# Two score passes moved in front of w_in and quads prepared one further ahead: cosine attention with a GELU MLP

## The chip, the cores and the metric

The kernel runs on one core of a Trainium2 chip. The metric is the device time of one execution in microseconds (us); the medians come from several executions. The profile is of one more execution, recorded by the hardware profiler. The engines are called PE (TensorE), DVE (VectorE), ACT (ScalarE), POOL (GpSimd) and SP (SyncE, which here only issues DMAs).

## What is computed

```python
# q, k, v: (8 batches, 12 heads, 448 positions, 64), tau = 0.1
q_n = q / (norm(q, axis=-1) + 1e-6)
k_n = k / (norm(k, axis=-1) + 1e-6)
attn = softmax(q_n @ k_n^T / tau)
x = concat_heads(attn @ v)              # (8*448, 768)
h = x @ w_in                            # (3584, 2048)
out = (0.5 * h * (1 + erf(h / sqrt(2)))) @ w_out   # (3584, 768)
```

Inputs and output are float32. The kernel multiplies in bfloat16 and accumulates in float32. Since the normalised scores are bounded by 1 / tau = 10, it takes exponentials without subtracting the maximum.

## The kernel before, in words

**Units of work.** Four heads of a batch make a quad, so a batch has NQ = 3 quads and the kernel 24 (numbered 0 to 23; batch b has quads 3b, 3b+1, 3b+2). Quad 0 is split in two, so unit numbers (`units`, line 112) are quad numbers plus one from quad 1 on.

**Preparation of a quad**, in steps over several engines: `load_qk` (line 122, two DMAs issued on SP), `square` (147, on POOL), `reduce` (158, on DVE: sums of squares), `logs` and `roots` (169 and 174, on ACT: square root as exp(0.5 ln)), `inverses` (183: an addition on POOL, a reciprocal on DVE), `scale` (200, two multiplications on POOL giving bfloat16), and `transposes` (214, one DMA transpose issued on SP into `qkT`). `root` (195) is logs, roots and inverses in a row. The three steps of a root work on a *group* of one or two units (`groups`, 114), so that one logarithm serves both. Buffers limit how far ahead a quad can be: `qk` has four, `qkb` and `qkT` three each, `sq` two.

**Attention of a batch.** A *pass* is one quad's scores for one chunk c of 64 keys for both head pairs (`scores`, 236: four quarter-array matmuls into a pair of PSUM banks), and its exponential on ACT (`exps`, 250). A quad has seven passes, a batch 21. There are three pairs of banks, 0, 1 and 2. `both` (325) ends a quad: `sums` (259, row sums by matmuls with ones, into the next of the two remaining banks), their transposition, inversion and spreading on DVE, `values` (278, attention times v, into one of the pairs), and `normalise` (321, on DVE, writes x).

**MLP of a batch.** `first` (630) multiplies x with w_in: 16 blocks m of 128 features with six matmuls (kd) each, and a Gelu on ACT for each block. The first `ahead` blocks run their first four kd before the last two, which need the last quad of x. Blocks sit in pairs of banks as `pairs` says, else in the two single banks in turn. Exponential and Gelu need different tables on ACT, so `first` loads the Gelu table at its start and the other at its end.

The second product is cut into pieces of 16 matmuls (`second_pieces`, 346), with a copy on DVE (line 356) and two stores on SP at the end. Pieces take the two single banks in turn, so a piece waits for the copy of the piece before the last. These matmuls, one at a time, are the `fill` of the next batch's attention: 96 in odd batches, 128 in even ones.

**The order of the work** is written out by hand: the program has a manual schedule, and each engine executes its instructions in the order in which the Python code issues them. `attention_first` (405) is the first batch. `attention(b, fill)` (584) alternates `run()`, which issues the next so many w_out matmuls of `plan`, with groups of passes (`group`, 578, from the table `group_pairs`: passes 3, 3, 3, 2, 3, 3, 2, 2, each with the pairs that it uses). The first group of a batch is issued at the end of `first` of the batch before. `upto(f, n)` (394) issues step f for all units below n that have not had it; where it stands decides where the step lies in its engine's queue.

Of the kernel before, what the change touches and what calls it, by code (L numbers as in the profile page):

```python
# [16 lines left out]
def kernel(  # L17
# [20 lines left out]
    NQ = H // 4  # L38
# [66 lines left out]
    def pair(i, name):  # L105
        pool = third[0] if i == 2 else ps_st
        return pool.tile([128, 2, 512], F32, tag=f"st{i}", name=name)
# [3 lines left out]

    units = [(0, 0, 1), (0, 1, 2)] + [(g, 0, 2) for g in range(1, NG)]
    NU = len(units)
    groups = [[n] for n in range(NQ + 2)] + [[NQ + 2, NQ + 3]]
    for n in range(2 * NQ + 1, NU, NQ):
        groups += [[n, n + 1], [n + 2]]
    shapes = [[len(gr), 2, units[gr[0]][2] - units[gr[0]][1], C] for gr in groups]
    place = {u: (n, j) for n, gr in enumerate(groups) for j, u in enumerate(gr)}
    qk_t, v_t, sq_t, nq_t, rn_t, qkb_t, qkT_t, pt_t = {}, {}, {}, {}, {}, {}, {}, {}
# [139 lines left out]
    def sums(g, chunks=range(C)):  # L259
        for c in chunks:  # L260
            if c == 0:
                bank_t[g, "sm"] = ps_acc.tile([128, 512], F32, tag="sm", name=f"sm{g}") if g < NQ else \
                    mm_tile(f"sm{g}", aside=0)
            for s in range(2):
                if g < NQ:
                    nc.tensor.matmul(bank_t[g, "sm"][64 * s:64 * (s + 1), :S],  # L266
                                     lhsT=ones2.rearrange("p a h r -> p (a h r)"), rhs=pt_t[g, s, c],
                                     start=(c == 0), stop=(c == C - 1), tile_position=(0, 64 * s))
                    continue

                half = 2
                for i in range(2) if c == half else ((c - (c > half)) % 2,):
                    r = 32 * (2 * s + i)
                    cols = slice(i * S // 2, (i + 1) * S // 2) if c == half else slice(0, S)
                    nc.tensor.matmul(bank_t[g, "sm"][r:r + 32, cols], lhsT=ones, rhs=pt_t[g, s, c][:, cols],  # L275
                                     start=(c < 2), stop=(c >= C - 2), tile_position=(0, r))
# [18 lines left out]
    def turned(g):  # L295
        tr = rcp.tile([128, NB, 32], F32, tag="tr", name=f"tr{g}")
        nc.vector.transpose(tr.rearrange("p b r -> p (b r)"), bank_t.pop((g, "sm"))[:, :S])  # L297
        bank_t[g, "tr"] = tr.rearrange("p b (k r) -> p k b r", k=2)

    def inverted(g):  # L300
        tr = bank_t.pop((g, "tr"))
        if g < NQ:
            su = tr[:, :, :, 0]
        else:


            for j in range(4):
                o = j ^ 1
                nc.vector.tensor_reduce(tr[32 * j:32 * (j + 1), :, :, 1], tr[32 * o:32 * (o + 1), :, :, 0:1],  # L309
                                        mybir.AxisListType.X, ALU.add)  # L310
            su = rcp.tile([128, 2, NB], F32, tag="su", name=f"su{g}")
            nc.vector.tensor_reduce(su, tr[:, :, :, 0:2], mybir.AxisListType.X, ALU.add)
        rc = bank_t[g, "rc"] = rcp.tile([128, 2, NB], F32, tag="rc", name=f"rc{g}")
        nc.vector.reciprocal(rc, su)

    def spread(g, h):
        rs = rcp.tile([128, NB, 32], F32, tag=f"rs{h}", name=f"rs{g}_{h}")
        nc.vector.transpose(rs, bank_t[g, "rc"][:, h].to_broadcast([128, NB, 32]))  # L318
        rs_t[g, h] = rs.rearrange("p b r -> p (b r)")
# [5 lines left out]
    def both(g, p):  # L325
        sums(g)
        turned(g)
        inverted(g)
        spread(g, 0)
        spread(g, 1)  # L330
        values(g, p=p)
        normalise(g, 0)
        normalise(g, 1)
# [60 lines left out]
    def upto(f, n, last=None):  # L394
        last = {load_qk: NG, load_v: NV, root: len(groups), load_wi: 4, load_wo: 4}.get(f, NU)
        while done.get(f, 0) < min(n, last):
            done[f] = done.get(f, 0) + 1
            f(done[f] - 1)
# [173 lines left out]
        done.update({square: 6, reduce: 5, root: 5, scale: 5, transposes: 5})  # L572


    passes = [(n, c) for n in range(NQ) for c in range(C)]
    group_pairs = [(0, 1, 2), (0, 1, 2), (0, 1, 2), (1, 2), (1, 2, 0), (1, 2, 0), (2, 0), (2, 0)]

    def group(b, k):
        n0 = sum(len(p) for p in group_pairs[:k])
        for p, (n, c) in zip(group_pairs[k], passes[n0:]):  # L580
            scores(b * NQ + n, ((0, c), (1, c)), p)
            exps(b * NQ + n, ((0, c), (1, c)))

    def attention(b, fill):
        fill = list(fill)
        plan = {96: (20, 13, 13, 12, 16, 22), 128: (24, 18, 20, 18, 22, 26)}[len(fill)]
        parts = iter(plan)

        def run():
            for _ in range(next(parts)):  # L590
                fill.pop(0)()

        x_t[b] = xp.tile([128, KD, S], BF16, tag="x", name=f"x{b}")
        g0, nu = b * NQ, (b + 1) * NQ + 1
        run()
        for n in (nu - 1, nu):
            upto(scale, n)
            upto(transposes, n)
        group(b, 1)
        upto(square, nu + 1)  # L600
        run()
        group(b, 2)
        both(g0, 0)
        upto(load_v, b + 3)
        if b == 1:
            upto(load_qk, g0 + NQ + 2)
        group(b, 3)
        upto(square, nu + 2)
        run()
        group(b, 4)  # L610
        upto(reduce, nu + 1)
        upto(load_qk, g0 + NQ + 3)
        run()
        group(b, 5)
        both(g0 + 1, 1)
        group(b, 6)
        run()
        group(b, 7)
        upto(reduce, nu + 2)
        n = 2 * b + 4  # L620
        if n < len(groups):
            logs(n)
            roots(n)
        run()
        both(g0 + 2, 1)
        if n < len(groups):
            inverses(n)
            done[root] = n + 1

    def first(b):  # L630
        sb, hf = divmod(b, 2)
        if hf == 0:
            g_t[sb] = gp.tile([128, KF, 2 * S], BF16, tag="g", name=f"g{sb}")
        nc.scalar.preload_act_table_set(GELU_SET)
        nu = (b + 1) * NQ + 1
        hps = {}
        pairs = (0, 2) if b else (0, 2, 6, 8)
        ahead = 4 if b else 5

        def mm(m, kds):  # L640
            for kd in kds:
                nc.tensor.matmul(hps[m], lhsT=wi[:, kd, m * 128:(m + 1) * 128],  # L642
                                 rhs=x_t[b][:, kd, :], start=(kd == 0), stop=(kd == KD - 1))

        def bank(m):
            if m in pairs:
                p = (2, 0)[m // 2] if b else (1, 0, 1, 0)[pairs.index(m)]
                st = pair(p, f"hp{b}_{m}")
                hps[m], hps[m + 1] = st[:, 0, :S], st[:, 1, :S]
            elif m not in hps:  # L650
                hps[m] = mm_tile(f"hp{b}_{m}")[:, :S]

        for m in range(ahead):
            bank(m)
            mm(m, range(KD - 2))
        if b == 0:
            upto(square, nu + 3)
        for n in (nu + 1, nu + 2) if b else (nu + 1,):
            upto(scale, n)
            upto(transposes, n)  # L660
        if b:
            upto(load_qk, (b + 1) * NQ + 5)
        else:
            upto(load_wo, 4)
        upto(square, nu + 3)
        upto(reduce, nu + 3)
        for m in range(ahead):
            mm(m, range(KD - 2, KD))
        for m in range(KF):
            if b == 0 and m == 8:  # L670
                for i in range(2):
                    transposes(4, i)
                    copies(4, i)
            if m >= ahead and (m == 0 or m - 1 not in pairs):
                for k in range(m, m + 1 + (m in pairs)):
                    bank(k)
                    mm(k, range(KD))
            nc.scalar.activation(g_t[sb][:, m, hf * S:(hf + 1) * S], hps.pop(m), AF.Gelu)  # L678
            if b == 0 and m == 5:
                nc.scalar.preload_act_table_set(EXP_SET)  # L680
                upto(root, 6)
                nc.scalar.preload_act_table_set(GELU_SET)
                upto(scale, nu + 2)
                upto(transposes, nu + 2)
                upto(load_qk, 2 * NQ + 1)
        if b + 1 < B:
            nc.scalar.preload_act_table_set(EXP_SET)
            group(b + 1, 0)
            upto(root, 2 * b + 6)

    upto(load_qk, 1)
    nc.scalar.preload_act_table_set(EXP_SET)
# [7 lines left out]
    fill = []  # L700
    for b in range(B):
# [12 lines left out]
        fill = [f for t, ni in todo if t not in tail for f in second_pieces(sb, t, ni)]  # L714
# [38 lines left out]
```

## Time and profile before

| | |
|---|---|
| median of 3 runs | 417.64 us (417.42 to 418.03) |
| the profiled execution | 418.57 us, span from first to last instruction 416.8 us |
| first batch's attention | 0 to 33.4 us |
| w_in of batches 0 and 1 | 33.4 to 52.5 and 80.6 to 98.9 us |
| one exponential of a pass | 917 ns, 168 of them |
| one Gelu | 547 ns, 128 of them |
| one square of a quad on POOL | 3.17 us |
| one reduction of a quad on DVE | 2.0 us |

Part 1 of the page has the busy time of each engine; part 4 the chain of work that ended last, followed back from the last instruction. [...] In the lists in order of time the first column is the start and the second the length, in us. An idle time in brackets names what ended it.

### The profile page before, as it was taken

The numbers are of one execution on the slowest core, as the hardware profiler recorded it, in microseconds if no ns is written. First come the engines' busy times: TensorE is split into PE (matmuls) and PEld (weight loads), VectorE is DVE, ScalarE is ACT, GpSimd is POOL, SyncE is SP. The second block draws the span as 40 slices with busy tenths as digits, with TensorE's granted clock in tenths as the row PEclk, the third lists the DMA queues.
The fourth block names the chain that finished last, engine by engine and source line by source line (L and its number), as shares of the span: only waits on it lengthen the run. The fifth ranks groups of instructions, "written<-read, shape, count | busy, mean of one in ns | idle before, by whom it ended". The sixth has DMA issues, their size and how long they took to land.

```text
span 416.8 us, 8254 instructions
## 1 busy us (share of the span) xinstructions
PE 409.3 (98%) x3506; PEld 212.1 (51%) x3506; DVE 188.3 (45%) x379; ACT 246.6 (59%) x358; POOL 167.3 (40%) x113
## 2 busy tenths in 40 slices
PE   7899999999999999999999999999999999999996
PEld 3344545555555554554555555455555554555564
DVE  5777228801676016741276314861167511661021
ACT  5995698356663578735865359735866348844300
POOL 4999706090900909053640636317280272000000
PEclk9999999999999999999999999999999999999999
DMA  8999999445473546729192382936375160430033
GB/s 288 263 259 205 204 215 258 115 81 186 91 185 77 92 174 92 187 60 242 18 233 65 77 228 43 195 77 126 141 135 180 38 90 0 85 75 2 0 77 76
DMA packets 66516, 54.53 MB, mean 131 GB/s; under 512 B 38576, under 2 KB 61488, under 8 KB 66480
## 3 DMA queue, kind: packets, MB, share of 16 engines
q1 hardware_dynamic: 53984, 41.79, 39.3%
q0 software_dynamic: 12112, 11.80, 17.8%
q8 instruction: 27, 0.44, 0.4%
q10 hardware_dynamic: 384, 0.43, 0.3%
q14 instruction: 9, 0.07, 0.1%
HBM read 45.61 MB, written 11.01 MB: 136 GB/s over the span
## 4 chain that ended last, share of the span: by engine, by line
PE 95%; DMA 2%; ACT 1%; DVE 1%; SPq 1%; issue 0%; DVEq 0%
PE hp L642 35%; PE op L352 35%; PE st L246 9%; PE o L289 8%; PE sm L275 4%; DMA qk<-in_q_dram 2%; PE op L367 1%; PE sm L266 1%; ACT pt L253 1%; SPq L129 1%; PE tp L225 0%; DVE qkT L230 0%; ACT sq L154 0%; DVE rn L192 0%; ACT root L178 0%
## 5 line engine op out<-in xcount | busy, mean ns | idle before, releaser
L253 ACT ACTIVATE pt<-st 128x896 bf16<-128x896 f32 x168 | 143.0, 917 | 39.6 <-PE st L246 38.7
L352 PE MATMUL op<-wo,g 128*128 128x384 bf16 x864 | 147.9, 327 | 0.0
L642 PE MATMUL hp<-x,wi 128*128 128x448 bf16 x768 | 146.8, 353 | 0.0
L678 ACT ACTIVATE g<-hp 128x448 bf16<-128x448 f32 x128 | 66.8, 547 | 99.3 <-PE hp L642 99.0
L352 PEld LDWEIGHTS <-g 128*128 128x128 bf16 x864 | 81.1, 98 | 63.2 <-issue 12.7
L642 PEld LDWEIGHTS <-wi 128*128 128x128 bf16 x768 | 74.4, 98 | 71.4 <-issue 2.9
L208 POOL TENSOR_TENSOR qkb<-qk,rn 128x896 bf16<-128x896 f32 (+1 forms) x49 | 79.7, 1652 | 47.1 <-DVE rn L192 47.1
L165 DVE TENSOR_REDUCE nq<-sq 128x28 f32<-128x1792 f32 (+2 forms) x30 | 48.8, 1637 | 64.6 <-POOL sq L156 61.3
L156 POOL TENSOR_TENSOR sq<-qk 128x1792 f32<-128x1792 f32 (+1 forms) x22 | 66.8, 3042 | 12.9 <-DMA qk<-in_k_dram 12.7
L356 DVE COPY ot<-op 128x384 f32<-128x384 f32 x54 | 29.5, 547 | 69.6 <-PE op L352 69.6
L190 POOL TENSOR_SCALAR se<-sr 128x28 f32<-128x28 f32 (+1 forms) x14 | 4.4, 313 | 122.7 <-ACT sr L181 122.7
L246 PE MATMUL st<-qkT 64*64 64x448 bf16 x672 | 48.3, 359 | 1.2 <-DVE qkT L230 1.0
L289 PE MATMUL o<-pt,v 64*64 64x448 bf16 x672 | 36.9, 352 | 0.0
L246 PEld LDWEIGHTS <-qkT 64*64 64x64 bf16 x672 | 18.2, 105 | 26.6 <-issue 18.3
L192 DVE RECIPROCAL rn<-se 128x28 f32<-128x28 f32 (+2 forms) x18 | 6.8, 376 | 51.4 <-POOL se L190 51.1
L318 DVE STREAM_TRANSPOSE rs<-rc 128x448 f32<-128x448 f32 x48 | 28.1, 623 | 0.8
L297 DVE STREAM_TRANSPOSE tr<-sm 128x448 f32<-128x448 f32 x24 | 15.6, 649 | 28.5 <-PE sm L275 25.4
L323 DVE TENSOR_TENSOR x<-o,rs 128x448 bf16<-128x448 f32 x48 | 27.0, 600 | 1.0 <-DVE rs L318 0.5
L289 PEld LDWEIGHTS <-v 64*64 64x64 bf16 x672 | 17.7, 106 | 15.8 <-issue 7.2
L275 PE MATMUL sm<-pt,ones 128*32 128x448 bf16 (+1 forms) x336 | 19.3, 332 | 0.0
L309 DVE TENSOR_REDUCE tr<-tr 32x28 f32<-32x28 f32 x84 | 16.5, 196 | 1.6
L275 PEld LDWEIGHTS <-ones 128*32 128x32 bf16 x336 | 7.4, 95 | 10.6 <-issue 8.9
(43 smaller groups left out, 118.5 us busy)
## 6 DMA issues: line engine op xcount, KB each, us to landing
out_dram<-ot SPq DMA_DIRECT2D x54, 192.0 KB, 2.7
qk<-in_q_dram SPq DMA_DIRECT2D x23, 448.0 KB, 6.3
qk<-in_k_dram SPq DMA_DIRECT2D x23, 448.0 KB, 7.0
v<-in_v_dram POOLq DMA_DIRECT2D x7, 672.0 KB, 10.8
wi<-in_moe_w_in_dram POOLq DMA_DIRECT2D x8, 384.0 KB, 14.3
wo<-in_moe_w_out_dram POOLq DMA_DIRECT2D x4, 768.0 KB, 14.0
qk<-in_q_dram SPq DMA_DIRECT2D x2, 224.0 KB, 3.6
v<-in_v_dram POOLq DMA_DIRECT2D x1, 448.0 KB, 9.5
```

The costliest lines, as they stand in the source:

```text
L156: eng.tensor_tensor(sq[:, part], t[:, part], t[:, part], ALU.mult)
L165: nc.vector.tensor_reduce(nq[:, part], sq[:, part], mybir.AxisListType.X, ALU.add)
L208: eng.tensor_tensor(qkb[:, i, :, s0:s1].rearrange("p c s d -> p s c d"), t[:, i, s0:s1], rn[:, i].to_broadcast([128, s1 - s0, C, D]), ALU. ...
L246: nc.tensor.matmul(st[cols, n, :S], lhsT=qkT[rows, 1, c, cols], rhs=qkT[rows, 0, :, cols], start=True, stop=True, tile_position=(64 * s, 6 ...
L253: nc.scalar.activation(pt[:, :m], st[:, :m, :S], AF.Exp, scale=inv_tau)
L275: nc.tensor.matmul(bank_t[g, "sm"][r:r + 32, cols], lhsT=ones, rhs=pt_t[g, s, c][:, cols], start=(c < 2), stop=(c >= C - 2), tile_position ...
L289: nc.tensor.matmul(bank_t[g, h][cols, :S], lhsT=v_t[g][rows, s, c, :], rhs=pt_t[g, s, c][rows], start=(c == 0), stop=(c == C - 1), tile_po ...
L318: nc.vector.transpose(rs, bank_t[g, "rc"][:, h].to_broadcast([128, NB, 32]))
L352: nc.tensor.matmul(ps[:, :NH], lhsT=g_t[sb][:, kf, t * 128:(t + 1) * 128], rhs=wo[:, kf, ni * NH:(ni + 1) * NH], start=(kf == 0), stop=(kf ...
L356: nc.vector.tensor_copy(ot[:, ni * NH:(ni + 1) * NH], ps[:, :NH])
L642: nc.tensor.matmul(hps[m], lhsT=wi[:, kd, m * 128:(m + 1) * 128], rhs=x_t[b][:, kd, :], start=(kd == 0), stop=(kd == KD - 1))
L678: nc.scalar.activation(g_t[sb][:, m, hf * S:(hf + 1) * S], hps.pop(m), AF.Gelu)
```

## The change

The passes of a batch b of 2 or more come in another order: two passes stand behind the values at the end of the attention of batch b - 1, in front of `first(b - 1)`; then follow, with w_out matmuls in between, 3, 3, 3, 3 with `both` and 2 more, and 3 with `both` and 2 more. In the words of the change, 2, 3, 3, 3, 5, 5. Batch 1 still begins with three passes behind `first(0)`, then 3, 3, 2, 3 with both and 2, 3 with both and 2. `plan` has other numbers of matmuls, as many runs as before. Quads 0 and 1 of a batch used to share a root; now the third quad of a batch and the first of the next do, and the second stands alone. The first quad of the next batch is scaled and transposed during the attention before, where it was done in `first`. In batch 1 a block of its own issues reduce, root, scale and transposes of quad 6 behind its third group of three passes, the one at the end of `first(0)` counted. In `first`, for b of 1 or more, blocks 0 and 1 take the single banks, blocks 2 to 5 take pairs 0 and 1, and six blocks run ahead instead of four.

```diff
-    groups = [[n] for n in range(NQ + 2)] + [[NQ + 2, NQ + 3]]
-    for n in range(2 * NQ + 1, NU, NQ):
-        groups += [[n, n + 1], [n + 2]]
+    groups = [[n] for n in range(NQ + 2)] + [[NQ + 2, NQ + 3], [2 * NQ + 1]]
+    for n in range(2 * NQ + 2, NU, NQ):
+        groups += [[n], [n + 1, n + 2] if n + 2 < NU else [n + 1]]
...
-    group_pairs = [(0, 1, 2), (0, 1, 2), (0, 1, 2), (1, 2), (1, 2, 0), (1, 2, 0), (2, 0), (2, 0)]
-
-    def group(b, k):
-        n0 = sum(len(p) for p in group_pairs[:k])
-        for p, (n, c) in zip(group_pairs[k], passes[n0:]):
+    at = {}
+
+    def visit(b, pairs):
+        for p in pairs:
+            n, c = passes[at.get(b, 0)]
+            at[b] = at.get(b, 0) + 1
             scores(b * NQ + n, ((0, c), (1, c)), p)
             exps(b * NQ + n, ((0, c), (1, c)))
...
-        plan = {96: (20, 13, 13, 12, 16, 22), 128: (24, 18, 20, 18, 22, 26)}[len(fill)]
+        plan = {96: (16, 14, 16, 18, 16, 16), 128: (20, 18, 20, 22, 32, 16)}[len(fill)]
...
-        g0, nu = b * NQ, (b + 1) * NQ + 1
+        g0, u = b * NQ, b * NQ + 1
         run()
-        for n in (nu - 1, nu):
-            upto(scale, n)
-            upto(transposes, n)
-        group(b, 1)
-        upto(square, nu + 1)
+        upto(scale, u + 3)
+        upto(transposes, u + 3)
+        if b == 1:
+            upto(load_qk, g0 + NQ + 2)
+            upto(square, u + 4)
+        visit(b, (0, 1, 2))
+        if b > 1:
+            upto(scale, u + 4)
+            upto(transposes, u + 4)
         run()
-        group(b, 2)
+        visit(b, (0, 1, 2))
+        if b == 1:
+            upto(reduce, u + 4)
+            upto(root, 2 * b + 5)
+            upto(scale, u + 4)
+            upto(transposes, u + 4)
+        run()
+        upto(load_qk, g0 + NQ + 3)
+        visit(b, (0, 1) if b == 1 else (0, 1, 2))
+        upto(square, u + 5)
+        run()
+        visit(b, (0, 1, 2))
         both(g0, 0)
         upto(load_v, b + 3)
-        if b == 1:
-            upto(load_qk, g0 + NQ + 2)
-        group(b, 3)
-        upto(square, nu + 2)
+        upto(load_qk, g0 + NQ + 4)
+        visit(b, (1, 2))
+        upto(reduce, u + 5)
         run()
-        group(b, 4)
-        upto(reduce, nu + 1)
-        upto(load_qk, g0 + NQ + 3)
-        run()
-        group(b, 5)
+        visit(b, (1, 2, 0))
         both(g0 + 1, 1)
-        group(b, 6)
-        run()
-        group(b, 7)
-        upto(reduce, nu + 2)
-        n = 2 * b + 4
+        visit(b, (2, 0))
+        n = 2 * b + 5
         if n < len(groups):
             logs(n)
             roots(n)
         run()
-        both(g0 + 2, 1)
+        both(g0 + 2, 2)
         if n < len(groups):
             inverses(n)
             done[root] = n + 1
+            visit(b + 1, (0, 1))
...
-        pairs = (0, 2) if b else (0, 2, 6, 8)
-        ahead = 4 if b else 5
+        pairs = {2: 0, 4: 1} if b else {0: 1, 2: 0, 6: 1, 8: 0}
+        ahead = 6 if b else 5
...
-        for n in (nu + 1, nu + 2) if b else (nu + 1,):
-            upto(scale, n)
-            upto(transposes, n)
-        if b:
+            upto(square, u + 3)
+            upto(scale, u + 1)
+            upto(transposes, u + 1)
+            upto(load_wo, 4)
+            upto(reduce, u + 3)
+        else:
+            upto(scale, u + 2)
+            upto(transposes, u + 2)
             upto(load_qk, (b + 1) * NQ + 5)
-        else:
-            upto(load_wo, 4)
-        upto(square, nu + 3)
-        upto(reduce, nu + 3)
+            upto(square, u + 4)
+            upto(reduce, u + 4)
...
-            group(b + 1, 0)
-            upto(root, 2 * b + 6)
+            if b == 0:
+                visit(1, (0, 1, 2))
+            else:
+                upto(root, 2 * b + 7)
```

More of the change, by code (lines that the diff above doesn't have):

```diff
@@ L634, in first @@
         nc.scalar.preload_act_table_set(GELU_SET)
-        nu = (b + 1) * NQ + 1
+        u = (b + 1) * NQ + 1
         hps = {}
-        pairs = (0, 2) if b else (0, 2, 6, 8)
-        ahead = 4 if b else 5
+        pairs = {2: 0, 4: 1} if b else {0: 1, 2: 0, 6: 1, 8: 0}
+        ahead = 6 if b else 5
         def mm(m, kds):
@@ L646, in bank @@
             if m in pairs:
-                p = (2, 0)[m // 2] if b else (1, 0, 1, 0)[pairs.index(m)]
-                st = pair(p, f"hp{b}_{m}")
+                st = pair(pairs[m], f"hp{b}_{m}")
                 hps[m], hps[m + 1] = st[:, 0, :S], st[:, 1, :S]
@@ L656, in first @@
         if b == 0:
-            upto(square, nu + 3)
-        for n in (nu + 1, nu + 2) if b else (nu + 1,):
-            upto(scale, n)
-            upto(transposes, n)
-        if b:
+            upto(square, u + 3)
[6 more added lines that the diff above has]
+            upto(transposes, u + 2)
             upto(load_qk, (b + 1) * NQ + 5)
-        else:
-            upto(load_wo, 4)
-        upto(square, nu + 3)
-        upto(reduce, nu + 3)
+            upto(square, u + 4)
+            upto(reduce, u + 4)
         for m in range(ahead):
@@ L682, in first @@
                 nc.scalar.preload_act_table_set(GELU_SET)
-                upto(scale, nu + 2)
-                upto(transposes, nu + 2)
+                upto(scale, u + 2)
+                upto(transposes, u + 2)
                 upto(load_qk, 2 * NQ + 1)
```

## The prediction

> **What bounds the kernel now.** I read the busy times first, then the chain that ended last, then that chain in order of time.
>
> ```profile
> PE 409.3 (98%) x3506; PEld 212.1 (51%) x3506; DVE 188.3 (45%) x379; ACT 246.6 (59%) x358; POOL 167.3 (40%) x113
> PE 95%; DMA 2%; ACT 1%; DVE 1%; SPq 1%; issue 0%; DVEq 0%
> ```
>
> TensorE is busy 98% of the span and 95% of the chain is its own. The waits of TensorE show none after 53 us. So from the second batch on nothing is gained by shortening another engine's work: time comes only from TensorE's own pauses between kinds of matmul, or goes if the change lets TensorE wait. The chain in order of time (start, length, what) shows these pauses; first an odd batch (96 w_out matmuls), then the last w_out pieces, then the second batch (b = 1).
>
> ```profile
> 147.99 2.27 PE hp L642 x12
> 150.26 0.69 PE st L246 x12
> 150.95 3.36 PE op L352 x20
> 154.31 0.82 PE st L246 x12
> 155.12 2.22 PE op L352 x13
> 157.34 0.72 PE st L246 x12
> 158.06 0.98 PE sm L275 x16
> ...
> 392.19 15.60 PE op L352 x96
> ```
>
> ```profile
> 53.18 3.36 PE op L352 x20
> 56.53 0.82 PE st L246 x12
> ```
>
> 96 w_out matmuls straight behind w_in take 15.60 us, 0.1625 each. Behind a score group 20 take 3.36, so 0.11 us is the way from quarter tiles to full ones. Three passes take 0.69 between w_out runs, where each pass alone is 0.187 (two take 0.38 directly behind values, 0.50 behind w_out): 0.13 is the way back. The first sums of a batch take 0.98 (1.01 in even batches) where later ones take 0.78: their last chunk waits for an exponential. The 0.82 is a third pass waiting for its PSUM pair.
>
> Second, what the moved preparation hangs on in batch 1, from the timelines of GpSimd, ScalarE and VectorE (start, length):
>
> ```profile
> 62.00 3.17 POOL L156 TENSOR_TENSOR sq<-qk 128x1792 f32<-128x1792 f32 x1 [11.26 <-DMA qk<-in_k_dram]
> 65.12 0.90 POOL L141 DMA_DIRECT2D v<-in_v_dram  x1
> ```
>
> ```profile
> 65.60 2.00 DVE L165 TENSOR_REDUCE nq<-sq 128x28 f32<-128x1792 f32 x1
> ```
>
> ```profile
> 103.19 0.33 ACT L172 ACTIVATE lq<-nq,tiny 128x28 f32<-128x28 f32 x1
> 103.61 0.23 ACT L181 ACTIVATE sr<-lq 128x28 f32<-128x28 f32 x1
> ```
>
> ```profile
> 103.92 0.28 POOL L190 TENSOR_SCALAR se<-sr 128x28 f32<-128x28 f32 x1 [10.03 <-ACT sr L181]
> ```
>
> ```profile
> 104.23 0.33 DVE L192 RECIPROCAL rn<-se 128x28 f32<-128x28 f32 x1 [8.29 <-POOL se L190]
> 104.48 0.49 DVE L356 COPY ot<-op 128x384 f32<-128x384 f32 x1
> ```
>
> GpSimd stood 11.26 us waiting for the load of quad 6 and could square it only at 62.00. Nothing waited for that before: the reduction stood behind both(3), the logarithm came at 76 us. The last five lines, of batch 2 and one fence for each engine, price the chain from logarithm to the next copy: 104.48 - 103.19 = 1.29 us.
>
> **What the Trainium skill says.** "Perfetto Trace Analysis", section on the Tensor Engine Instruction: ACT, DVE and GPSIMD are strict FIFO. The trace agrees: the copy at 104.48 belongs to a piece whose 16th matmul was done at 99.51 + 2.6 = 102.1, and sat behind the waiting reciprocal. "TensorE: Matmul & The Clock Gate", section "Wait — 56ns, not 53.3ns?": a warm matmul takes N / 2.4 GHz + 2.5 ns, 162.5 for N = 384; the trace has 162.5. Same page, "What's actually happening": after an idle window of about 3.4 us, free-running, the clock is halved until it was busy for one. The kernel's first 20 spin matmuls take 5.86 us (1.93 to 7.79) instead of 20 x 0.189 = 3.78, which fits; no later idle stretch in this trace shows a restart.
>
> **The change, part by part.**
>
> *Batches 2 to 7, order of the passes.* No matmul is added or removed. Two passes now stand behind the values of the batch before (0.40 instead of a group of their own), w_out follows w_in directly, and six stretches of quarter tiles per batch replace seven. Odd batch before: scores 0.69 + 0.82 + 0.72 + 0.38 + 0.79 + 0.69 + 0.42 + 0.50 = 5.01, sums 0.98 + 2 x 0.78, values 3 x 1.45, w_out 16.25, in all 28.15. After: five triples 3.45, pairs 0.42 + 0.42 + 0.40, sums 3 x 0.78, values 4.35, w_out 96 x 0.1625 + 5 x 0.11 = 16.15: 27.53. That is -0.62. Even batch (128) the same way: 33.11 to 32.73, -0.38 (there the triples waited for nothing). The last batch has no successor: -0.62 - 0.40 = -1.02. Sum: 3 x 0.38 + 2 x 0.62 + 1.02 = **-3.40 us**.
>
> Does the new order bring new waits there? Exponentials take 2.54 per triple (0.85 each); the shortest distance between triples is 0.69 + 14 x 0.1625 + 0.11 = 3.08, enough. Sums of a batch's first quad now come five passes after its last score. The two early exponentials hold pairs 0 and 1: the first is done about 1.3 us after its scores, while w_in reaches pair 0 after 0.40 + 8 x 0.189 + 0.11 = 2.0; pair 1 at 3.5 against 2.15. The table load of 1.28 still ends before the first Gelu, since w_in now runs six blocks of four (24 x 0.189 = 4.5 us) before it needs the last quad. Nearest to the edge is the bank of sums(1) in odd batches, which the next w_out piece takes: the turned read follows 2.0 of reduction and 0.5 of copy, and I get 0.35 us to spare. Cost zero; without that cover up to 0.3 in two batches.
>
> *Preparation of batches 2 to 7.* The two squares (3.17 each), two reductions and four scales (1.66 each) fit in the same order: root at A + 2.6 (A: end of w_in), scales done at A + 10.2, the transposes of the next batch's first quad need old scores that end at A + 6.5 and are needed at A + 27. On SP the output stores and loads stand behind these transposes until about A + 12; three output tiles are enough for three (or, over 33 us, four) row blocks. Zero.
>
> *Batch 1.* Here reduce, root and scale of quad 6 are put straight behind this stage's second triple (the batch's third), and its load is not moved: SP issues it at 52.75 behind the same transposes, among the same traffic, so the square still starts at **62.00**. VectorE reaches the reduction at about 59, directly behind the copy of the first w_out piece, and stands: 65.12 square done, reduction 65.17 to 67.19, logarithm 67.23, + 1.29 is 68.52 for the copy of the second piece, + 0.49 and the signal: 69.06. Queued behind it on VectorE are all copies of w_out pieces; on ScalarE the exponentials wait behind the logarithm until 67.9. TensorE: 53.18 + 2.71 (16 w_out) = 55.89; the triple ends at 57.35 as before (same exponentials); 14 w_out 2.39: 59.73; triple 60.42; 16 w_out 63.13; pair 0.50: 63.63; the last two of the third piece 0.43: 64.07. The fourth piece takes the bank of the second, free at 69.06: a **stall of 4.99 us**. From there 2.60 + 0.69 + 0.78 + 1.45 + 0.42 + 2.71 + 0.69 + 0.78 + 1.45 + 0.42 + 2.71 + 0.78 + 1.45 + 0.40 leads to 86.39, where the stage ended at 80.62: **+5.77**, of it 0.78 for the two extra passes and the wait of the first triple.
>
> *Clock after the stall.* Not shown by this trace in the middle of a run. Below: 0. Above: 2.1 us, what the cold start cost. A gain is excluded. With a free-running window of 3.4 us, a stall of 5.0 holds a whole one in (5.0 - 3.4) / 3.4 = 47% of the cases (an estimate from that page), so I take 1.0.
>
> **Sum.** -3.40 + 5.77 + 1.0 = +3.4 us. The profiled execution took 418.57 (span 416.8), 0.93 above the median 417.64; on it the sum gives 422.0, on the median **421.0**. The span should be about 420.2.
>
> **The rivals.**
>
> *A, faster: the load is in time.* If the landing of quad 6 moves forward, the stall shrinks one to one. From landing to freed bank it is 69.06 - 62.00 = 7.06, and TensorE comes at 64.07, so the point is a landing at 57.0. Then -3.40 + 0.78 = -2.6: 415.0. Against: its issue at 52.75 waits for the same transposes, and the DMA queues hold the same traffic up to there. 10%.
>
> *B, slower still: the pauses don't go.* If each new junction costs what the old one did (0.11 and 0.13 are moved, or the 0.35 margin isn't there), only the stall is left: +5.8, 423.4, with the clock up to 425. For it: the small waits of before were also invisible in the plan. Against: w_out behind w_in without a pause is in the trace. 12%.
>
> *C, the change of order isn't what ends last:* half of the stall is hidden, for instance by a landing at 59.5, and both effects cancel: 417.6. 4%.
>
> **Numbers.** Forecast 74%, its own range 419.6 (clock 0, stall 4.6) to 422.4 (clock 2.1, and little else). The range 418.6 to 423.5 takes in most of B and leaves out A and C. About 0.2% (0.8 us) can be told from no change here. Faster 0.10, same 0.04, slower 0.86.
>
> **What would show it.** Right: in batch 1 one idle gap of TensorE of about 5 us before a w_out matmul, released by the copy of line 356; VectorE idle before the reduction for about 6 us, released by the square; w_out directly behind w_in without 0.69 between; first sums of 0.78. Wrong: a square of quad 6 that starts before 57 us; a logarithm that doesn't hold back exponentials; new waits of TensorE in batches 2 to 7; w_in waiting for pairs 0 or 1.

## The result and the profile after

The changed kernel takes 422.93 us (median of 6, 421.35 to 423.87), the kernel before 417.69: ratio 1.0118, 95% interval 1.0093 to 1.0142. It is slower, by 5.2 us; 421.0 was forecast, within 418.6 to 423.5. One run of all that follow, at 424.12 us in e6, was in a slower state of the chip and is left out of its figures.

The profiled execution after has a span of 421.9 us (before 416.8). From the page, parts 1 and 4:

```profile
PE 408.9 (97%) x3506; PEld 213.1 (51%) x3506; DVE 188.6 (45%) x380; ACT 246.6 (58%) x360; POOL 167.0 (40%) x114
PE 85%; POOL 4%; DMA 4%; DVE 2%; ACT 2%; SPq 1%; issue 1%; POOLq 0%; DVEq 0%
```

The same TensorE work in a longer span, and the chain that ended last now runs for 15% through other engines. The waits of TensorE behind 53 us name the place:

```profile
PE op L352 <- DVE ot L356: 5.3, 1, 5.3
PE st L246 <- DMA qkT<-qkb: 0.6, 1, 0.6
PE st L246 <- ACT pt L253: 0.4, 1, 0.4
```

One wait of 5.3 us, for a copy of a w_out piece. The chain in order of time (start, length, what) shows what that copy waited for:

```profile
52.06 10.21 DMA qk<-in_k_dram
...
62.39 3.18 POOL sq L156
...
65.60 2.03 DVE nq L165
...
67.66 0.33 ACT lq L172
...
68.01 0.23 ACT sr L181
...
68.32 0.29 POOL se L190
...
68.63 0.33 DVE rn L192
68.96 0.42 DVE ot L356
...
69.42 5.17 PE op L352 x16
74.59 0.69 PE st L246 x12
```

The load of quad 6 lands, GpSimd squares, VectorE reduces, and a round trip over ScalarE and GpSimd leads to the reciprocal; only then comes the copy, whose piece was done eight microseconds before. VectorE's own timeline shows that it had nothing else to do:

```profile
55.16 0.56 DVE L356 COPY ot<-op 128x384 f32<-128x384 f32 x1 [10.90 <-PE op L352]
65.60 2.02 DVE L165 TENSOR_REDUCE nq<-sq 128x28 f32<-128x1792 f32 x1 [9.89 <-POOL sq L156]
68.63 0.33 DVE L192 RECIPROCAL rn<-se 128x28 f32<-128x28 f32 x1 [1.01 <-POOL se L190]
68.88 0.95 DVE L356 COPY ot<-op 128x384 f32<-128x384 f32 x2
```

It stood 9.89 us in front of the reduction, with two copies behind it. And the 16 matmuls after the gap take 5.17 us where 16 take 2.60 (below). These are distances between starts: one w_out matmul is printed as 0.33 us long, while the next starts 0.16 us after it. The table of stages gives the reason: its columns are busy times and counts of five engines, then the granted TensorE clock, DMA share and GB/s.

```profile
64.00:66.00 2.00, 0.10 (x1) 0.00 (x0) 0.40 (x1) 0.00 (x0) 1.57 (x1) 1.00 0.66 204
66.00:68.00 2.00, 0.00 (x0) 0.00 (x0) 1.62 (x1) 0.32 (x1) 0.00 (x0) 0.88 0.57 205
68.00:70.00 2.00, 0.58 (x2) 0.25 (x2) 1.20 (x3) 1.84 (x3) 1.17 (x2) 0.50 0.00 0
70.00:72.00 2.00, 2.00 (x8) 0.97 (x7) 0.00 (x0) 0.00 (x0) 2.00 (x2) 0.50 0.00 0
72.00:74.00 2.00, 2.00 (x8) 0.99 (x7) 0.00 (x0) 0.00 (x0) 2.00 (x2) 0.50 0.17 32
74.00:76.00 2.00, 2.00 (x34) 0.60 (x33) 0.56 (x1) 1.04 (x2) 2.00 (x2) 0.91 1.21 211
```

The clock is halved from about 67.5 us (0.88 over two microseconds is 0.5 for 0.48 of them) to 74.4. From batch 2 on all is as planned; an odd batch after:

```profile
158.50 2.60 PE op L352 x16
161.10 0.69 PE st L246 x12
161.79 2.38 PE op L352 x14
164.17 0.69 PE st L246 x12
...
171.98 0.78 PE sm L275 x16
...
185.60 0.38 PE st L246 x8
```

w_out follows w_in without a pause (16 in 2.60), the triples shown take 0.69, the first sums 0.78, and the two early passes 0.38.

### The profile page after: what moved, and what is told of

It is laid out like the page before. It is cut to its first block, busy times and chain, and to the rows that moved or that the text cites. A ratio compares the mean times of both kernels' runs of the same rounds, so it can differ in the third digit from the quotient of the medians.

```text
span 421.9 us, 8255 instructions
## 1 busy us (share of the span) xinstructions
PE 408.9 (97%) x3506; PEld 213.1 (51%) x3506; DVE 188.6 (45%) x380; ACT 246.6 (58%) x360; POOL 167.0 (40%) x114
## 4 chain that ended last, share of the span: by engine, by line
PE 85%; POOL 4%; DMA 4%; DVE 2%; ACT 2%; SPq 1%; issue 1%; POOLq 0%; DVEq 0%
PE op L352 33%; PE hp L652 30%; PE st L246 8%; PE o L289 8%; PE sm L275 4%; DMA qk<-in_k_dram 2%; POOL qkb L208 2%; DMA qk<-in_q_dram 2%; POOL sq L156 1%; PE op L367 1%; DVE nq L165 1%; PE sm L266 1%; ACT pt L253 1%; SPq L129 1%; DVE rn L192 0%
## 5 line engine op out<-in xcount | busy, mean ns | idle before, releaser
L352 PE MATMUL op<-wo,g 128*128 128x384 bf16 x864 | 150.4, 330 | 5.3 <-DVE ot L356 5.3
L352 PEld LDWEIGHTS <-g 128*128 128x128 bf16 x864 | 82.3, 99 | 69.1 <-issue 18.4
L652 PEld LDWEIGHTS <-wi 128*128 128x128 bf16 x768 | 74.4, 98 | 71.4 <-issue 2.9
L688 ACT ACTIVATE g<-hp 128x448 bf16<-128x448 f32 x128 | 65.9, 545 | 66.3 <-PE hp L652 66.0
L275 PE MATMUL sm<-pt,ones 128*32 128x448 bf16 (+1 forms) x336 | 17.8, 332 | 0.0
L403 PE MATMUL spin<-blank,ident 128*128 128x448 bf16 x34 | 9.6, 426 | 2.1 <-DVE root L89 1.9
## 6 DMA issues: line engine op xcount, KB each, us to landing
wi<-in_moe_w_in_dram POOLq DMA_DIRECT2D x8, 384.0 KB, 15.2
```

The costliest lines, as they stand in the source:

```text
L352: nc.tensor.matmul(ps[:, :NH], lhsT=g_t[sb][:, kf, t * 128:(t + 1) * 128], rhs=wo[:, kf, ni * NH:(ni + 1) * NH], start=(kf == 0), stop=(kf ...
```

## The experiments

The theory: the changed order gains about 3.5 us in batches 2 to 7, and loses more in batch 1 alone, because two steps of quad 6 are put into VectorE's queue before their data can be there. The rivals: the new order itself makes TensorE wait in batch 1; ScalarE's held-back exponentials are the cause; or where the passes stand gains nothing. All times below are medians; a ratio, with its 95% interval, is against the kernel before on the same chip, and is not exactly the quotient of two medians.

**Early load** (e1). The load of quad 6 is issued by ScalarE at the second Gelu block of batch 0.

```diff
-    def load_qk(g):
+    def load_qk(g, by=None):
...
-                eng = nc.scalar if g == 0 and s0 == 0 and i == 1 else nc.sync
+                eng = by or (nc.scalar if g == 0 and s0 == 0 and i == 1 else nc.sync)
...
+            if b == 0 and m == 1:
+                load_qk(2 * NQ, nc.scalar)
+                done[load_qk] = 2 * NQ + 1
...
-                upto(load_qk, 2 * NQ + 1)
```

> The changed kernel with one edit: the two loads of quad 6 are issued by ScalarE during the second Gelu block of the first w_in stage (about 39 us) instead of by SP behind a DMA transpose (about 51.5 us). Theory (reduce and root of quad 6, put too early for that load, block VectorE in order, and with it the copy that frees the bank of the next w_out piece): the landing moves to about 50 us, before the point of 57; the idle gap of 5.33 us and the 2.57 us at half speed behind it vanish, so about 7.9 us less than the changed kernel: 415.0 us, faster than the kernel before by about 0.6%. Rival (the new order itself makes TensorE wait in batch 1, whatever the load): the gap stays, 422 to 423 us. Rival (the load is moved into busier traffic and delays w_out): the gap becomes a wait for a weight load, between the two.

Measured: 419.27 us, 1.0030 (1.0019 to 1.0042). The wait for the copy is gone. VectorE and TensorE now read:

```profile
55.97 2.01 DVE L165 TENSOR_REDUCE nq<-sq 128x28 f32<-128x1792 f32 x1
```

```profile
PE st L246 <- DMA qkT<-qkb: 2.7, 1, 2.7
```

VectorE no longer stands in front of the reduction: 3.7 of the 7.9 us are won. But what the third rival of this run said came true in another place: the DMA transposes of quad 4, issued behind that load, land at 62.30 us and TensorE waits 2.7 us for them, then runs slowly for a while (16 matmuls in 3.7 us).

**A busy gap** (e2). Unused matmuls where TensorE would stand idle.

```diff
+        if b == 1:
+            plan = (16, 14, 16, 16, 16, 16)
...
+        if b == 1:
+            for _ in range(2):
+                fill.pop(0)()
+            busy = pair(2, "busy")
+            for _ in range(26):
+                nc.tensor.matmul(busy[:, 0, :S], lhsT=ident, rhs=blank, start=True, stop=True)
         run()
```

> The changed kernel with 26 unused full-array matmuls (26 x 0.189 = 4.9 us) put where TensorE stands idle in batch 1, into a pair of banks that is free there. The wait for the copy stays. Theory (the 16 w_out matmuls behind the gap ran in 5.17 instead of 2.60 us because TensorE had stood idle): the wait still ends at about 69.4 us, the 16 matmuls take 2.6 us, and the time is 2.6 us below a changed kernel that was slowed, 420.4 to 421 us, with less spread between runs. Rival (those matmuls are slow for want of operands, or for the copy that runs beside them): they stay at 5.2 us and the time at 423.

Measured: 420.43 us (419.79 to 421.27), 1.0067 (1.0054 to 1.0080). The timeline of TensorE, start and length:

```profile
62.82 5.08 PE L625 MATMUL busy<-blank,ident 128*128 128x448 bf16 x26
67.97 2.76 PE L352 MATMUL op<-wo,g 128*128 128x384 bf16 x16
70.66 0.76 PE L246 MATMUL st<-qkT 64*64 64x448 bf16 x12
```

The bank comes free at 67.9 us, after 5.1 us without useful matmuls (in this run the square began 1.45 us earlier than in the changed kernel's), the 16 matmuls take 2.69 us, and 2.5 us of the loss are gone. The mean granted clock is 0.999 or 1.000 in all five runs, where it was 0.992 to 0.996 in the six of the changed kernel. So about a third of the 7.9 us was not the gap but the clock behind it.

**Root later** (e3). Only the reduction stays at its place.

```diff
             upto(reduce, u + 4)
-            upto(root, 2 * b + 5)
-            upto(scale, u + 4)
-            upto(transposes, u + 4)
...
         both(g0, 0)
+        if b == 1:
+            upto(root, 2 * b + 5)
+            upto(scale, u + 4)
+            upto(transposes, u + 4)
```

> The changed kernel with only the reduction of quad 6 left at its place; root, scale and transposes of it stand behind the first both of the batch. Theory (VectorE's queue is what blocks, first at the reduction, then 1.3 us more at the reciprocal that waits for ScalarE and GpSimd): the copy is free 1.3 us earlier, the gap is about 4.0 instead of 5.3 us, the time 421.6 us if the clock still falls, 419 if it doesn't. Rival (exponentials held back by the logarithm on ScalarE are what TensorE waits for): without the logarithm there the gap is gone, 415 to 416 us.

Measured: 428.22 us, 1.0247 (1.0229 to 1.0265). The waits of TensorE:

```profile
PE st L246 <- DMA qkT<-qkb: 5.5, 1, 5.5
PE op L352 <- DVE ot L356: 3.9, 1, 3.9
```

The gap for the copy is 3.9 us, as the theory said: about 1.4 us of the 5.3 were the round trip, 3.9 the reduction. With no logarithm in ScalarE's queue 3.9 us of the gap stay, so the second rival falls as its main cause. The total I missed: quad 6 is now ready so late that the two early passes of batch 2 wait 5.5 us for it. Quad 6 has a narrow place: too early, and VectorE stands; too late, and its passes do.

**The same step in the kernel before** (e5). One line is added in front of the first `both` of batch 1, which moves the reduction there.

```diff
         group(b, 2)
+        if b == 1:
+            upto(reduce, nu + 1)
         both(g0, 0)
```

> The kernel before with one line moved: the reduction of quad 6 stands in front of the first both of batch 1 instead of behind its next group. Theory (a step put into VectorE's queue ahead of its data blocks what stands behind it, whatever the order of the passes): VectorE stands from about 60 to 65.2 us, the transposition of the sums starts at 67.2 instead of 61.3, x of that quad is written about 5.9 us later, and the triple that needs its pair of banks waits about 6 us: 423 to 424 us, and up to 426 with TensorE at half speed behind the gap. Rival (only the new order makes that place critical): under 1 us, 418 us.

Measured: 426.92 us, 1.0210 (1.0194 to 1.0226); TensorE:

```profile
PE st L246 <- DVE x L323: 5.8, 1, 5.8
```

The wait is 5.8 us (6 expected), through another buffer: here the pair of banks whose values VectorE had not normalised. The total is 0.9 us above the most that was expected. The first rival falls as the cause of the gap: a reduction ahead of its data costs this in the old order too, and e1 has the new order without that gap.

**Passes back behind w_in** (e4), on top of the early load.

```diff
-            visit(b + 1, (0, 1))
...
             else:
+                visit(b + 1, (0, 1))
                 upto(root, 2 * b + 7)
```

> The kernel with the early load, and the two passes of the next batch back behind its w_in stage instead of in front (batches 2 to 7). Theory of the gain: each batch gets back one way from full to quarter tiles and one from quarter to full, 0.12 + 0.11 us, six times: 1.4 us more than the early load, 416.4 us; the shorter first sums and triples stay. Rival (the gain comes from the earlier exponentials, which spare waits later): triples wait again for pairs, 2 to 3.5 us more. Rival (no gain from the order at all): the same time.

Measured: 420.86 us (419.69 to 422.91), 1.0074 (1.0052 to 1.0096); +1.6 against the early load, but the wait for quad 4 and the clock behind it vary between runs. The three runs of e4 with a mean clock of 0.999 or 1.000 took 419.69 to 420.10 us, the two such runs of the early load 417.56 and 417.63: 2.3 us less. The profiles are steadier. From the start of w_in of batch 1 to that of batch 7 it is 85.82 to 378.29 = 292.47 us, with the passes in front 85.18 to 374.88 = 289.70: 2.8 us, of which 0.38 are two passes counted in the stage before. An odd batch begins like this:

```profile
155.30 0.54 ACT g L687
155.86 1.28 ACT L698
157.15 1.73 ACT pt L253 x2
...
158.93 0.57 PE st L246 x8
159.50 2.38 PE op L352 x14
```

So the gain of the two early passes has two parts, 2.4 us together: 0.23 us per junction, and in odd batches 0.34 us in which a triple waits for exponentials that stand behind the last Gelu and a table load. The first I had counted; the second lies in my "triples" term. Over the same stretch the kernel before takes 293.30 us (80.62 to 373.92), so about 0.8 us more come from the rest of the new order; no run takes these apart.

**Late w_out** (e6), **the same with the passes behind** (e7), **the same loads in the kernel before** (e8). On top of the early load, the second half of w_out is issued ten microseconds later, to leave the transposes of quad 4 alone.

```diff
         upto(transposes, u + 3)
         if b == 1:
+            upto(load_wo, 4)
...
-            upto(load_wo, 4)
```

> The kernel with the early load of quad 6, and the second half of w_out loaded later: GpSimd issues it behind the last scale of quad 5 (about 50 us) instead of before its roots (about 40 us). Theory (in the early-load kernel the DMA transposes of quad 4 were late, 62.30 instead of 59.88 us, because quad 6 and w_out were in front of them): the transposes land before their passes need them at about 59.3 us, the gap of 2.69 us and about 1 us at half speed go: 415.4 us, 0.5 to 0.6% faster than the kernel before. Rival (w_out is then late for its fourth piece at about 64 us): TensorE waits for w_out, 417 to 420 us. Rival (the order itself costs what the load did): 419 us as before.

> The kernel with the early load and the late w_out, and the two passes back behind w_in in batches 2 to 7. Theory of the gain: six junctions of 0.23 us, and in odd batches 0.34 us more where a triple waits for exponentials behind the table load, as the profile with the early load alone showed: 2.4 us more than with the passes in front, 417.8 us, the time of the kernel before. Rival (no gain from where the two passes stand): the same time as with the passes in front.

> The kernel before with the same two edits of the loads (quad 6 early, second half of w_out late) and none of the new order. Theory (the gain of the last version lies in the order of the passes, not in the loads): nothing in the kernel before waited for either load, so 417.7 us, no difference. Rival (the loads themselves gain): about 415.5 us.

Measured: e6 418.58 us (417.12 to 421.52), 1.0021 (1.0005 to 1.0038); e7 422.22, 1.0093 (1.0069 to 1.0118); e8 423.75, 1.0130 (1.0106 to 1.0154). TensorE in e6 and in e8:

```profile
PE op L352 <- DMA wo<-in_moe_w_out_dram: 2.1, 1, 2.1
```

```profile
PE op L352 <- DMA wo<-in_moe_w_out_dram: 3.1, 1, 3.1
```

The rival of e6 came true: TensorE waits for w_out. The load it waits for lands at 67.57 us, 16.2 us after the end of its issue. In e8 the same load takes 19.3 us and lands at 70.0, so the wait is 3.1 us: "nothing waited for either load" did not hold once w_out moved, since issued at 40 us it is in time and at 50 us it is not. From 40 to 62 us the transfers leave little room: quad 6 moved forward made the transposes of quad 4 late (e1), and w_out moved back to spare them came late itself. e7 misses its 417.8 by 4.4 us for the same reason: it waits 2.4 us for w_out and then has half its clock for 3.4 us. In the profiles, e7 against e6 repeats the cost of the passes behind (292.48 against 289.70 us).

**Steps later** (e9), **with the passes behind** (e10). The loads are those of the changed kernel; only the queue places of quad 6 in batch 1 differ. `both` gets a step to run behind its two spreads.

```diff
-    def both(g, p):
+    def both(g, p, between=lambda: None):
...
         spread(g, 1)
+        between()
...
-        if b == 1:
-            upto(reduce, u + 4)
-            upto(root, 2 * b + 5)
-            upto(scale, u + 4)
-            upto(transposes, u + 4)
         run()
...
         visit(b, (0, 1) if b == 1 else (0, 1, 2))
+        if b == 1:
+            upto(reduce, u + 4)
...
         visit(b, (0, 1, 2))
-        both(g0, 0)
+        if b == 1:
+            logs(2 * b + 4)
+            roots(2 * b + 4)
+            both(g0, 0, lambda: inverses(2 * b + 4))
+            done[root] = 2 * b + 5
+            upto(scale, u + 4)
+            upto(transposes, u + 4)
+        else:
+            both(g0, 0)
```

> The changed kernel with its loads untouched and only the steps of quad 6 in batch 1 moved in their queues: the reduction behind the next pair of passes (so that VectorE first copies the second w_out piece), logarithm and root behind the triple in front of the first both, the reciprocal between the spreads and the normalisation of that both, scale and transposes behind it. Theory (what costs 7.9 us is only that VectorE stood in front of that copy): the square still starts at about 62 us, the copy no longer waits for it, the gap of 5.3 us and the slow matmuls behind it are gone: 415.3 us, 0.6% faster than the kernel before. The transposes then land about 80 us, one microsecond before their passes; if they come late, the gap is there and the time 416 to 418 us. Rival (batch 1 is bound by its transfers in any order): another wait of 2 to 3 us appears, 418 to 419 us, as with the two edits of the loads.

> The kernel with the steps of quad 6 moved in their queues, and the two passes back behind w_in in batches 2 to 7. Theory of the gain: 0.23 us per junction and 0.34 us more in odd batches, 2.4 us in all, as the profiles of the two versions with the early load showed: 417.7 us, level with the kernel before. Rival (where the two passes stand gains nothing): the same time as with the passes in front.

Measured: e9 421.98 us, 1.0095 (1.0073 to 1.0116); e10 418.07, 1.0003 (0.9995 to 1.0011). TensorE in e9:

```profile
PE st L246 <- DMA qkT<-qkb: 4.4, 1, 4.4
PE sm L275 <- DVE ot L357: 0.6, 1, 0.6
```

The wait for a copy has shrunk from 5.3 to 0.6 us (it now stands at the first sums, which take the next bank), but the transposes of quad 6, issued at 74.91, land at 84.93, 4.4 us after their passes could start, and w_in behind them runs slowly (20.83 instead of 18.27 us). They should have landed at about 80 us; beside the loads of v and of quad 9, issued within the next 3.4 us, they took 10.0. So e9 misses its 415.3 by 6.7 us. e10, whose passes stand behind w_in, doesn't meet that wait: 418.07 (417.7 expected), level with the kernel before.

**In front from batch 3 on** (e11), and **with a later reduction** (e12). From e9, the two passes of batch 2 alone go behind w_in; e12 also puts the reduction behind the fourth run of w_out.

```diff
-            visit(b + 1, (0, 1))
+            if b > 1:
+                visit(b + 1, (0, 1))
...
             else:
+                if b == 1:
+                    visit(2, (0, 1))
                 upto(root, 2 * b + 7)
```

> The kernel with the steps of quad 6 moved in their queues, and the two passes in front of w_in from batch 3 on; those of batch 2, whose quad 6 is not there in time, stay behind w_in. Theory (two separate things: a gain of 0.4 to 0.6 us per batch wherever the next quad is ready, and in batch 1 a quad that can't be ready): no wait for the transposes of quad 6 and none for the copy of the second w_out piece; against the version with all passes behind, 0.23 + 0.57 a pair of batches and 0.95 in the last come back, 2.5 us: 415.5 us, 0.55% faster than the kernel before. Rival (each gain in one batch returns as a wait in another): 417.9 us.

> As the version with passes in front from batch 3 on, but with the reduction of quad 6 one stretch of w_out later, behind the copies of the third and fourth piece. Theory: the wait of 0.6 us of the first sums of batch 1 for a copy behind that reduction goes, 414.9 us. Rival (the transposition of the sums, behind the reduction now, holds a pair of banks until the next triple): the same 415.5 or up to 0.5 more.

Measured: e11 416.23 us, 0.9948 (0.9931 to 0.9965); e12 416.25, 0.9959 (0.9943 to 0.9975). Both are faster than the kernel before, by 0.4 to 0.5%. From e10 to e11 only the passes of batches 3 to 7 move in front of w_in, and 1.8 us are won (2.2 expected). e12 doesn't gain on e11: the wait of 0.6 us for a copy that e9 had is gone, and 0.5 us for a pair of banks stands in its place, as its rival said. (The profile of e11 shows neither wait; its TensorE came to batch 1 3.6 us later.) All that TensorE still waits for in e12 behind 50 us:

```profile
PE st L246 <- DVE x L323: 0.5, 1, 0.5
PE st L246 <- ACT pt L253: 0.4, 1, 0.4
```

The medians are 0.7 and 1.4 us above what was expected; the runs spread more (e11 415.41 to 418.53, e12 415.59 to 419.62). In the profile of e11 TensorE has half its clock from 16.4 to 23.2 us, in batch 0, and w_in of batch 0 ends 3.6 us later than in e12; in e12 it has not. No edit touches that stretch, and three of the 38 runs of the kernel before that were timed beside these have a lowered mean clock too (0.991 to 0.995), at 420.28 to 421.72 us. What starts it is open.

## Why the prediction was right

- *The bound.* Behind 53 us TensorE sets the end everywhere before, and everywhere but in batch 1 after. Confirmed by its waits: nothing behind batch 1.
- *Batches 2 to 7.* -3.40 us was forecast. From the end of w_in of batch 1 to the start of that of batch 7 it was 98.89 to 373.92 before and 107.55 to 378.99 after: -3.59. An odd batch lost 0.65 (0.62), an even one 0.42 (0.38), the last 1.02 (1.02). The two early passes take 0.38, where I had put 0.40. No new wait came, so rival B is out, though its 423.4 us is nearer to the measured 422.93 than the forecast is.
- *The stall.* 4.99 us were forecast from a square at 62.00 and a copy free at 69.06; the square started at 62.39 and the piece at 69.42: 5.33. Cause, place and size hold; e1, e3, e5 and e9 show the cause from four sides. Rivals A and C are out for this kernel, as the load did not move; e1 shows that A's condition (a landing before 57 us) does free the copy, but not that it gives A's 415.0 us.
- *VectorE's idle time* I read wrongly: it reaches the reduction at 55.72 us and not at about 59, since the first piece's 16 matmuls were done at 55.9 by my own sum, and stands 9.89 us instead of about 6. The stall doesn't depend on it, as the square ends it either way.
- *The clock.* The term that was mis-sized. I took 1.0 us, as 2.1 us in about half of the cases; the profiled run shows 5.10 us between starts where 2.60 would do, 2.5. Neither the size nor the share held. The bound came from the first spins of the kernel, and the granted clock on record reads 1.00 there, so that the record doesn't show how much of a slow time they saw. And all six runs paid: four have a mean clock of 0.992, which is what 6.83 us at half speed make of 421.9 us, and the two at 421.35 and 421.61 us have 0.995 and 0.996, about what 3.41 us would make (an estimate from these figures).
- *Not foreseen:* 0.8 us in the third triple of batch 1, which waited for the transposes of quad 4 (0.61 idle). I had taken their landing for granted because nothing waited for it before. This run's TensorE reached that point 0.6 us earlier than the old one, and they landed 0.3 us later (59.8 instead of 59.5). The wait cost nothing in the end, for the copy comes free by the date of the load: time that TensorE loses or wins ahead of the stall only makes the stall shorter or longer. That it came to the stall at 64.09, as forecast (64.07), is luck: a start 0.77 us shorter and this wait cancel.

The sum, from the profiles: w_in of batch 1 started at 89.28 us, where 86.39 and 1.0 for the clock were forecast. Of these 1.9 us the later square makes 0.4 and the clock 1.5. Batches 2 to 7 gave 0.2 back, and the span was 421.9 instead of 420.2. So the direction, the place and the two large terms were right, and the time lies in the upper part of the range. It lies above 422.4, the end that I gave the forecast alone; the wide range had been drawn to take in rival B, which is not what happened. That the range held is in part luck.

## What to carry to other kernels

A step moved ahead in an in-order queue is only as early as its data: look up when the last of its inputs lands, and what stands behind it in that queue, before its own cost. In a kernel bound by TensorE, a gap there can cost its length and then the slow clock behind it (here 5.3 and 2.5 us), so a single late step in one batch can outweigh a gain in six. When a pipeline is set one unit further ahead, look at its first round by itself, since nothing was prepared for it: here the kernel became faster than before, by 1.9 us, when that round kept its two passes behind w_in and the steps of quad 6 stood where their data are (e11).

## What the runs showed of the hardware

- *The price of a gap on TensorE.* After 5.33 us of idling (from 64.09) the granted clock fell to 0.50 about 3.4 us into the gap and came back 6.8 us later; 16 matmuls cost 2.5 us more. After 3.9 us (e3) it was at 0.50 for about 3.4 us, and 16 matmuls took 4.37 us, 1.8 more. 26 matmuls without use in the gap (e2) kept the clock at 1.00. Of the ten stretches at half clock in all profiles, five lasted 3.41 us (e1, e3 twice, e4, e7) and five 6.83, twice that (the changed kernel, e5, e8, e9, e11), whatever the gap.
- *How long a gap must be.* The Trainium skill, "TensorE: Matmul & The Clock Gate", section "What's actually happening", names a free-running window of about 3.4 us, and half the clock after at least one idle window. The lengths agree with that window. The condition does not: in e1 a gap of 2.69 us (59.61 to 62.30) was enough, and in e7 one of 2.40, while one of 2.14 (e6) left the profiled run at 1.00. So the share of cases that the prediction worked out from a whole idle window had no ground in this kernel. The stages of e1, with the clock as the third number from the right; it falls at about 61.8 and is back at 65.2:

```profile
60.00:62.00 2.00, 0.00 (x0) 0.00 (x0) 0.00 (x0) 0.58 (x1) 0.00 (x0) 0.96 1.34 101
62.00:64.00 2.00, 1.70 (x11) 0.62 (x12) 0.00 (x0) 1.05 (x2) 0.00 (x0) 0.50 1.18 288
64.00:66.00 2.00, 2.00 (x11) 1.01 (x9) 0.47 (x2) 1.10 (x3) 0.28 (x1) 0.69 0.96 338
```

- *DMA transposes beside loads.* The transposition of one quad lands 4.0 us after its issue in the quiet part of the kernel before (the median there), and 10.0 us after it in e9, in a stretch of 16 us in which 2 MB were moved. Those of quad 4, in the busy stretch around 50 us, took 12.0 us in the kernel before, 13.1 after the change and 15.2 in e1. A place in the order that rests on the quiet figure fails in a busy stretch.
